# Tile 0 in written order on ScalarE, VectorE and POOL, with five weight-conversion steps per slot

## The chip, the cores and the metric

The kernel runs on one core of a Trainium2 chip. The core has five engines with a queue of instructions each: TensorE (PE; its weight loads are listed as PEld), VectorE (DVE), ScalarE (ACT), GpSimd (POOL) and SyncE (SP), which issues the DMAs. Each queue is fixed when the kernel is compiled and is worked off in its order. An instruction that waits for another engine holds what is queued behind it. The metric is the device time of one execution in microseconds.

## The reference

Three layers follow each other on 4352 tokens of width 128, all in float32.

```
phi(x)  = outer product of x@S1.T and x@S2.T            (8 x 8 = 64 features)
attn    = (phi(q) @ (phi(k).T @ v)) / (phi(q) @ sum(phi(k)) + 1e-6)   per batch and head
x       = attn / sqrt(mean(attn^2) + 1e-6) * rms_g
y       = (silu(x @ w_gate) * (x @ w_val)) @ w_out       d_ff = 1536
out     = soft mixture of 8 experts x 4 slots over all 4352 rows of y
```

Some inputs (S1, S2, w_gate, w_val and w_out) come as 64-bit floats and are handed to the kernel as pairs of 32-bit words, so that the kernel converts them to float32 on the chip.

## The kernel before

**Tiles and slots.** The rows are cut into nine tiles, eight of 512 rows and one of 256. The feed-forward layer of a tile runs over `NF = 12` slices of d_ff of 128 columns; one slice of one tile is a slot (`for i in range(n_slots + LAG)`, L947). In a slot `ff_in` (L637) makes the gate product g and the value product v on TensorE, three matmuls of 512 columns each: the high part of the weight (L621), its low part (L622), and the low part of x (L623). `ff_gate` (L647) does the silu on ScalarE and the product with v on VectorE. `ff_out` (L668), two slots later (`LAG`), multiplies with w_out into the tile's sum o. In tile 0 `ff_out` is one float32 matmul from unsplit weights, recorded as two pieces of L676; from tile 1 on it is three matmuls from split weights (L621 to L623 again), with the split of the gated value in `ff_high` and `ff_low`. The PSUM tiles of g and of v have two buffers each, so slot i+2 writes g only when the silu of slot i has read it, and v only when the gate product of slot i has.

**Weight conversion.** The weights come in nine groups in the order gv0, o0, gv1, gv2, o1, gv3, gv4, o2, gv5; a gv group serves two slots, an o group four. Converting a group takes six steps (`f64_words`, L184): ScalarE takes the absolute value of the high word (L189) and scales the low word (L192); VectorE does max, shift and or (L194, L196, L198); POOL adds the two (L202, in two pieces of 256 columns). A gv group has two more steps (`split_w`, L230): ScalarE rounds the high part (L238) and POOL subtracts it, which gives the low part wgl (L244, two pieces). The o groups get these two steps later, in `split_o`, which is appended in slot 9.

**The front.** Before the first slot `front` (L847) issues the steps of the string `FRONT` (attention for batch 0, tile 0's x, and the first 22 conversion steps) in that order on all four engines. 44 conversion steps are left for the slots: two of gv1, six of gv2, six of o1, eight of gv3, eight of gv4, six of o2 and eight of gv5. Each slot issues up to `CONV` of them.

**Order.** `in_order` (L836) runs a step, puts each of its instructions behind the latest recorded instruction of its own engine, and then records the step's last instruction of each engine in `ordered`. The edge is one of queue order and not a wait. With `ordered` and `latest` empty it does nothing, and the order on each engine is chosen by a planner, which places what its own model of the costs holds to be ready. Before, both are cleared in slot 0, so that the planner orders the slots; only conversion and chain steps of the first `LOCK = 3` slots are put behind the front (`after_front`, L892).

**Chains.** Beside the slots run generators that advance a step at a time, at two places of a slot (POST, after the gate, and PE, after `ff_out`). `q_chain(1)` makes tile 1's x: transpose L492 in slot 0, the outer products L282 and the transpose L508 in slot 1, the divides in slots 3 and 4, four squares on ScalarE and the root on POOL (L566, L567) in slot 5, the scaling L571 in slot 6, `parts` (L581, L582) in slot 8. `k_chain(1)` starts in slot 8 with POOL work (memset L324, copies L347), then transposes, projections (L354) and outer products for the keys of batch 1. `make_own` (L791 on) is POOL work that is written in tile 2.

Of the kernel before, what the change touches and what calls it, by code (L numbers as in the profile page):

```python
# [21 lines left out]
NF = DFF // P  # L22
# [12 lines left out]
qt n:4 c:1 c:1 c:1 qx kr c:2 c:2 c:2 c:2 c:2 c:2 c:3 c:3  # L35
"""

CONV = 8
LOCK = 3

WHOLE = NF
# [7 lines left out]
def body(ctx, tc, q, k, v, s1, s2, wg, wv, wo, rg, phi, w1, w2, out):  # L49
# [199 lines left out]
    def split_o():  # L249

        for i, w in enumerate(wo32):
            yield from split_w(("o", i), w, pool)
# [384 lines left out]
    def ff_in(T, f):  # L637
        w = 512 if T < 8 else 256
        for store, tag in ((gps, "g"), (vps, "v")):
            store[T, f] = [ps.tile([P, 512], F32, tag=tag, name=tag, bufs=2) for _ in pieces(T, f)]  # L640
        for e, (c, cs) in enumerate(chunks(T, f)):
            for m, store in enumerate((gps, vps)):
                o = store[T, f][e % len(store[T, f])]
                sl = slice(P * c, P * c + P)
                gate[0] = mm3(o[:, cs], wgh[:, m, sl], wgl[:, m, sl], xh[T][:, 0:w], xl[T][:, 0:w], True, True)
# [41 lines left out]
    def r_chain(T):  # L687
        x2 = row("x2")
        act.copy(x2, ops.pop(T))
        yield PE, 0  # L690
        a = aux()
        for t in range(4):
            pe.matmul(a[32 * t : 32 * t + 32, 0:P], phi_sb, x2[:, P * t : P * t + P], start=True, stop=True)
        b = aux()
        for t in range(4):
            pe.transpose(b[:, P * t : P * t + P], x2[:, P * t : P * t + P], ident)
        yield POST, 1
        lT = sb.tile([P, P], F32, tag="lT", name="lT")
        act.copy(lT, a[:, 0:P])
        act.copy(x2n[:, 4 * T : 4 * T + 4, 0:DM], b.rearrange("p (t d) -> p t d", d=DM))  # L700
        yield PE, 0
        a = aux()
        pe.transpose(a[:, 0:P], lT, ident)
        yield POST, 1
        dve.tensor_reduce(out=mcol[:, T : T + 1], in_=lT, op=ALU.max, axis=AX.X)
        dve.tensor_copy(lg[:, 4 * T : 4 * T + 4, :], a[:, 0:P].rearrange("p (t s) -> p t s", s=NS))
        if T >= 6:
            for i in range(3 if T == 6 else 1):
                yield POST, 1
                less_max(slice(8 * i, 8 * i + 8) if i < 3 and T == 6 else slice(4 * T, 4 * T + 4))  # L710
            if T == 6:
                yield POST, 1
                less_max(slice(24, 28))
# [40 lines left out]
    def a_max():  # L754

        m1 = sb.tile([P, 1], F32, tag="m1", name="m1")
        dve.tensor_reduce(out=m1, in_=mcol, op=ALU.max, axis=AX.X)
        a = aux()
        pe.transpose(a[0:1, 0:P], m1, ident)
        mr = sb.tile([P, P], F32, tag="asb", name="mr", bufs=3)[0:1].rearrange("p (t s) -> p t s", s=NS)  # L760
        m0 = a[0:1, 0:P].rearrange("p (t s) -> p s t", s=NS)
        dve.tensor_reduce(out=mr[:, 0], in_=m0, op=ALU.max, axis=AX.X)
        dve.tensor_copy(mr[:, 1:4], mr[:, 0:1].to_broadcast([1, 3, NS]))
        a = aux()
        pe.matmul(a[:, 0:NS], ones, mr[:, 0], start=True, stop=True)
        pe.matmul(a[:, NS : NS + 1], mr.rearrange("p t s -> p (t s)"), ones[:, 0:1], start=True, stop=True)
        A["m"] = sb.tile([P, 1], F32, tag="am", name="am")
        dve.tensor_copy(A["m"], a[:, NS : NS + 1])
        A["b"] = sb.tile([P, NS], F32, tag="siT", name="amb")
        dve.tensor_copy(A["b"], a[:, 0:NS])  # L770
# [43 lines left out]
    def spawn(c, phase, at=0):  # L814
        chains.append([c, phase, now + at])
# [18 lines left out]
    latest, ordered = {}, list(ENGINES)  # L834

    def in_order(step, *args):  # L836
        traced = nc.cur_bb.bb.instructions
        start = len(traced)
        with ExitStack() as s:
            for i in latest.values():  # L840
                s.enter_context(tc.issue_after(i))
            step(*args)
        for i in traced[start:]:
            if i.engine in ordered:
                latest[i.engine] = i
# [46 lines left out]
    def after_front():  # L892
        s = ExitStack()
        if now < base + LOCK:
            for i in front_end.values():
                s.enter_context(tc.issue_after(i))
        return s
# [49 lines left out]
    for i in range(n_slots + LAG):  # L947
        now = base + i
        if i < n_slots:
            T, f = slots[i]  # L950
            ff_in(T, f)
            if f == 0:
                start_tile(T)
        if i == NF - 3:
            conv.append(split_o())
        if i == 0:
            ordered.clear()
            latest.clear()
        if 1 <= i <= n_slots:
            in_order(ff_low, *slots[i - 1])  # L960
        if i < n_slots:
            in_order(ff_gate, T, f)
        for c in list(chains):
            with after_front():
                in_order(advance, POST, c)
        for _ in range(CONV):
            with after_front():
                in_order(conv_step, 1)
        if i < n_slots:
            in_order(ff_high, T, f)  # L970
        if i >= LAG:
            To, fo = slots[i - LAG]
            in_order(ff_out, To, fo)
            if fo == NF - 1 and To < 8:
                if To < 7:
                    spawn(r_chain(To), POST, 1)
                else:
                    with tc.high_priority():
                        for _ in r_chain(To):
                            pass  # L980
                        a_max()
        for c in list(chains):
            with after_front():
                in_order(advance, PE, c)
# [223 lines left out]
```

## Time and profile before

| | |
|---|---|
| median of three runs | 327.0 us (326.41 to 327.06) |
| profiled execution, its own time | 326.61 us |
| span of the profiled execution | 324.8 us |
| TensorE busy | 312.0 us, 96% |
| VectorE busy | 237.5 us, 73% |
| ScalarE busy | 185.4 us, 57% |
| POOL busy | 61.2 us, 19% |

The span is the time from the first to the last instruction; the profiled execution's own time has 1.8 us around it. Busy shares are means over the whole span and hide the stage that is changed: slot 0 begins at 23.35 us, and the last `ff_out` of tile 0 ends at 67.84 us. TensorE's durations are modelled at their ends; a 512-column matmul shows 0.39 us as a row, while the next one starts 0.23 us later.

### The profile page before, as it was taken

How to read it: one execution, taken by the hardware profiler on the slowest of the kernel's cores; microseconds unless marked ns; L12 is line 12 of the kernel's file. 1: busy time of each engine (PE TensorE's matmuls, PEld its weight loads, DVE VectorE, ACT ScalarE, POOL GpSimd, SP SyncE). 2: the span in 40 equal slices, each digit the busy share in tenths (PEclk: the TensorE clock that was granted, in tenths of full speed). 3: DMA queues.
4: the chain of work that ended last, by engine and by line, in shares of the span. 5: the costliest groups of instructions: out<-in, count | busy, mean ns of one | idle time of the engine just before them, and what ended most of it. 6: DMA issues, size and time to landing. Idle time of an engine off the chain costs nothing.

```text
span 324.8 us, 5533 instructions
## 1 busy us (share of the span) xinstructions
PE 312.0 (96%) x2028; PEld 248.1 (76%) x2028; DVE 237.5 (73%) x458; ACT 185.4 (57%) x412; POOL 61.2 (19%) x104
## 2 busy tenths in 40 slices
PE   8987989999998999999999999999999999999994
PEld 6774655778886878888888778888888878897574
DVE  4779976775878785777887868678778666664663
ACT  3757464456565455665564657565656666556553
POOL 3356699700010210001001000010020100003030
PEclk9997899999999999999999999999999999999998
DMA  8988000000007000000070000000890394000007
GB/s 201 297 289 206 0 0 1 2 0 2 0 0 199 7 2 0 2 0 0 2 198 5 3 0 2 0 0 6 279 251 3 78 339 103 0 2 0 2 3 274
DMA packets 31131, 22.40 MB, mean 69 GB/s; under 512 B 13056, under 2 KB 27136, under 8 KB 31104
## 3 DMA queue, kind: packets, MB, share of 16 engines
q1 hardware_dynamic: 31072, 22.04, 23.6%
q8 instruction: 16, 0.26, 0.3%
q14 instruction: 11, 0.09, 0.1%
q10 hardware_dynamic: 32, 0.00, 0.0%
HBM read 19.81 MB, written 2.23 MB: 68 GB/s over the span
## 4 chain that ended last, share of the span: by engine, by line
PE 75%; issue 6%; DVE 5%; DMA 1%; POOL 1%; ACT 1%; DVEq 0%; SPq 0%; POOLq 0%
PE v L621 6%; PE g L621 6%; PE v L622 6%; PE g L622 6%; PE v L623 6%; PE g L623 6%; PE o L621 6%; PE o L622 6%; PE o L623 6%; PE aux L520 3%; PE aux L384 2%; PE aux L354 2%; PE aux L497 2%; PE o L676 2%; PE fo L1159 1%
## 5 line engine op out<-in xcount | busy, mean ns | idle before, releaser
L651 ACT ACTIVATE silu<-g 128x512 f32<-128x512 f32 (+1 forms) x103 | 60.5, 592 | 41.1 <-PE g L623 38.6
L661 ACT CAST hh<-hf 128x512 fp32r<-128x512 f32 x89 | 55.0, 617 | 42.3 <-DVE hf L652 38.8
L666 DVE TENSOR_TENSOR hl<-hf,hh 128x512 fp32r<-128x512 f32 x89 | 60.9, 685 | 22.4 <-ACT hh L661 21.0
L652 DVE TENSOR_TENSOR hf<-v,silu 128x512 f32<-128x512 f32 (+1 forms) x91 | 61.8, 680 | 19.7 <-PE v L623 9.5
L621 PE MATMUL v<-xh,wgh 128*128 128x512 f32 (+1 forms) x108 | 44.0, 408 | 2.1 <-DVE hh L652 1.6
L621 PE MATMUL g<-xh,wgh 128*128 128x512 f32 (+1 forms) x108 | 42.8, 402 | 1.0 <-ACT wgh L238 1.0
L622 PE MATMUL g<-xh,wgl 128*128 128x512 f32 (+1 forms) x108 | 42.7, 395 | 0.0
L622 PE MATMUL v<-xh,wgl 128*128 128x512 f32 (+1 forms) x108 | 42.1, 390 | 0.0
L623 PE MATMUL g<-xl,wgh 128*128 128x512 f32 (+1 forms) x108 | 41.4, 384 | 0.0
L623 PE MATMUL v<-xl,wgh 128*128 128x512 f32 (+1 forms) x108 | 41.0, 381 | 0.0
L621 PE MATMUL o<-hh,woh 128*128 128x512 f32 (+1 forms) x94 | 36.8, 392 | 0.0
L623 PE MATMUL o<-hl,woh 128*128 128x512 f32 (+1 forms) x94 | 36.6, 389 | 0.0
L622 PE MATMUL o<-hh,wol 128*128 128x512 f32 (+1 forms) x94 | 35.7, 380 | 0.0
L566 POOL TENSOR_SCALAR rs<-ss 128x4 f32<-128x4 f32 (+1 forms) x9 | 2.6, 290 | 138.8 <-ACT sq L561 137.2
L621 PEld LDWEIGHTS v<-xh,wgh 128*128 128x128 f32 x108 | 20.6, 190 | 8.7 <-DVE hh L652 3.8
L621 PEld LDWEIGHTS g<-xh,wgh 128*128 128x128 f32 x108 | 20.3, 191 | 5.8 <-ACT wgh L238 1.9
L622 PEld LDWEIGHTS g<-xh,wgl 128*128 128x128 f32 x108 | 20.6, 191 | 4.7 <-issue 0.8
L622 PEld LDWEIGHTS v<-xh,wgl 128*128 128x128 f32 x108 | 20.3, 188 | 4.7 <-issue 1.3
L623 PEld LDWEIGHTS g<-xl,wgh 128*128 128x128 f32 x108 | 20.6, 191 | 4.3 <-issue 0.5
L623 PEld LDWEIGHTS v<-xl,wgh 128*128 128x128 f32 x108 | 20.3, 188 | 4.6 <-issue 0.7
L621 PEld LDWEIGHTS o<-hh,woh 128*128 128x128 f32 x94 | 17.7, 188 | 3.0
L623 PEld LDWEIGHTS o<-hl,woh 128*128 128x128 f32 x94 | 17.7, 188 | 3.0
(254 smaller groups left out, 522.2 us busy)
## 6 DMA issues: line engine op xcount, KB each, us to landing
ring<-in_moe_w_dram SPq DMA_DIRECT2D x12, 256.0 KB, 6.5
ring<-in_moe_w_dram SPq DMA_DIRECT2D x5, 512.0 KB, 5.4
ring<-in_k_dram SPq DMA_DIRECT2D x8, 256.0 KB, 3.0
qt<-in_q_dram SPq DMA_DIRECT2D x4, 512.0 KB, 5.3
ring<-in_v_dram SPq DMA_DIRECT2D x16, 128.0 KB, 4.7
ring<-in_moe_w_gate_dram SPq DMA_DIRECT2D x6, 256.0 KB, 6.3
ring<-in_moe_w_val_dram SPq DMA_DIRECT2D x6, 256.0 KB, 6.5
ring<-in_moe_w_out_dram SPq DMA_DIRECT2D x3, 512.0 KB, 6.2
```

What stands on the lines that cost most here:

```text
L354: pe.matmul(o, self.kT[g][:, P * t : P * t + pp], bdf, start=True, stop=True)
L384: pe.matmul(self.a["kv", hp][64 * h2 : 64 * h2 + D1, 64 * hp : 64 * hp + 64], va[:, h, 2 * i + g, :] if t < 8 else vr[:, h, :], self.pk[hp ...
L497: pe.matmul(self.a["q"][:, 64 * h : 64 * h + 64], self.qD[:, P * h : P * h + P], bdf, start=True, stop=True)
L520: pe.matmul(o, pD[:, f, h, :], rhs, start=(f == 0), stop=(f == 1))
L621: first = pe.matmul(o, ah, bh, start=start, stop=False)
L622: pe.matmul(o, al, bh, start=False, stop=False)
L623: last = pe.matmul(o, ah, bl, start=False, stop=stop)
L651: mark["silu"] = act.activation(s[:, cs], g[:, cs], AF.Silu).ins
L652: mark["gate", T, f] = dve.tensor_tensor(out=hf32[T, f][:, cs], in0=v[:, cs], in1=s[:, cs], op=ALU.mult).ins
L661: act.copy(hh[T, f], hf32[T, f])
L666: dve.tensor_tensor(out=hl[T, f], in0=hf32.pop((T, f)), in1=hh[T, f].bitcast(F32), op=ALU.subtract)
L676: last = pe.matmul(ops[T][:, 0:w], w_c, h[:, cs], start=(c == 0), stop=(c == NF - 1))
```

## The change

In slot 0 only TensorE is taken out of the recorded order. ScalarE, VectorE and POOL go on in written order until slot 12, the first of tile 1, where both tables are cleared. So in slots 0 to 11 each of these three queues holds, slot by slot: the silu or gate product, then what the chains issue at POST, then the conversion steps, then what the chains issue at PE. `CONV` falls from 8 to 5, so the 44 steps end in slot 8 in place of slot 5. No instruction is added or removed.

```diff
-CONV = 8
+CONV = 5
 LOCK = 3
...
         if i == NF - 3:
             conv.append(split_o())
         if i == 0:
+            ordered.remove(mybir.EngineType.PE)
+            latest.pop(mybir.EngineType.PE)
+        if i == NF:
             ordered.clear()
             latest.clear()
         if 1 <= i <= n_slots:
             in_order(ff_low, *slots[i - 1])
         if i < n_slots:
             in_order(ff_gate, T, f)
         for c in list(chains):
             with after_front():
                 in_order(advance, POST, c)
         for _ in range(CONV):
             with after_front():
                 in_order(conv_step, 1)
```

## Rows read from the trace of the kernel before

**Rows 1.** The page's 40 slices: TensorE's busy tenths and its granted clock.

```profile
PE   8987989999998999999999999999999999999994
PEclk9997899999999999999999999999999999999998
```

**Rows 2.** Busy time of each engine in four stretches of tile 0.

```profile
core 0: us, PE busy (x) PEld busy (x) DVE busy (x) ACT busy (x) POOL busy (x), PEclk, DMA share, GB/s
28.90:35.70 6.80, 6.17 (x11) 3.69 (x12) 6.77 (x13) 2.65 (x6) 3.06 (x6) 0.50 0.41 83
35.70:44.30 8.60, 8.50 (x38) 5.33 (x36) 8.50 (x15) 4.48 (x8) 7.55 (x10) 1.00 0.00 0
44.30:61.20 16.90, 15.13 (x63) 9.99 (x63) 10.88 (x16) 8.52 (x23) 16.02 (x23) 1.00 0.00 0
61.20:67.80 6.60, 6.60 (x27) 4.76 (x27) 5.30 (x10) 3.27 (x7) 1.85 (x10) 1.00 0.01 2
```

**Rows 3.** POOL's timeline (start, us, work), from gv5's add on.

```profile
52.05 1.42 POOL L202 TENSOR_TENSOR cvt<-cvs,cvc 128x256 uint32<-128x256 uint32 x2 [0.46 <-POOL rs L566]
53.41 0.98 POOL L324 MEMSET kvz<- 128x1056 f32 x1
...
55.46 1.02 POOL L567 TENSOR_TENSOR rs<-rs,mhalf 128x4 f32<-128x4 f32 x1
56.44 1.86 POOL L244 TENSOR_TENSOR wol<-ring,woh 128x256 fp32r<-128x256 f32 x2
...
59.65 1.43 POOL L244 TENSOR_TENSOR wgl<-cvt,wgh 128x256 fp32r<-128x256 f32 x2
```

**Rows 4.** TensorE's timeline at the stalls (in brackets the idle time before).

```profile
27.23 1.10 PE L497 MATMUL aux<-bd,T 128*128 128x64 f32 x8 [0.86 <-DVE T L492]
29.00 1.22 PE L621 MATMUL g<-xh,wgh 128*128 128x512 f32 x2 [0.67 <-ACT wgh L238]
...
55.00 1.03 PE L621 MATMUL g<-xh,wgh 128*128 128x512 f32 x2
...
58.48 1.00 PE L354 MATMUL aux<-bd,T 128*128 128x64 f32 x8
...
59.99 1.36 PE L354 MATMUL aux<-bd,T 128*128 128x64 f32 x10 [0.30 <-ACT T L342]
61.28 0.50 PE L622 MATMUL g<-xh,wgl 128*128 128x512 f32 x1
...
66.82 1.02 PE L676 MATMUL o<-hh,ring 128*128 128x512 f32 x2
```

**Rows 5.** The chain that ended last, two pieces: start, us, what.

```profile
54.24 0.23 PE v L622
...
54.70 0.86 PE o L676 x2
```

**Rows 6.** VectorE's timeline: conversion steps without and with POOL at work.

```profile
25.86 0.69 DVE L198 SCALAR_TENSOR_TENSOR cvs<-ring,cvt 128x512 uint32<-128x512 uint32 x1
...
31.47 0.41 DVE L194 TENSOR_SCALAR ring<-ring 128x512 f32<-128x512 f32 x1
...
48.57 0.93 DVE L194 TENSOR_SCALAR cvt<-cvt 128x512 f32<-128x512 f32 x1 [1.88 <-ACT cvt L189]
...
50.42 1.11 DVE L198 SCALAR_TENSOR_TENSOR cvs<-ring,cvt 128x512 uint32<-128x512 uint32 x1
```

**Rows 7.** Groups by shape, 23.3 to 67.8 us: busy us, mean ns, idle before.

```profile
L202 POOL TENSOR_TENSOR cvt<-cvs,cvc 128x256 uint32<-128x256 uint32 x10 | 8.2, 841 | 6.9 <-DVE cvs L198 3.7 <-ACT woh L238 2.0 <-DVE rd L536 0.7
L651 ACT ACTIVATE silu<-g 128x512 f32<-128x512 f32 x14 | 8.0, 595 | 6.8 <-PE g L623 4.8 <-DVE hh L652 1.9
L652 DVE TENSOR_TENSOR hh<-v,silu 128x512 f32<-128x512 f32 x12 | 7.9, 679 | 1.5 <-PE v L623 1.4
...
L244 POOL TENSOR_TENSOR wgl<-cvt,wgh 128x256 fp32r<-128x256 f32 x10 | 7.7, 791 | 0.0
...
L189 ACT ACTIVATE cvt<-ring 128x512 f32<-128x512 f32 x5 | 3.3, 669 | 1.8 <-POOL wgl L244 1.8
```

## The prediction, made before the changed kernel ran

> **What bounds the kernel now.** I read the page's slices first [rows 1]: TensorE is busy nearly throughout, and its granted clock dips only in the fourth and fifth slice and at the end. From tile 1 on TensorE sets the pace, so a change confined to tile 0 is worth what it makes TensorE lose there. Next the windows [rows 2]. From 28.9 to 35.7 us the granted clock is 0.50, the 1.2 GHz level, ahead of which TensorE had idled 0.86 and 0.67 us with only small matmuls between [rows 4]. VectorE is full to 44.3, then POOL, 16.0 of 16.9 us. From 61.2 TensorE is full at 2.4 GHz. So tile 0 is held by the conversion, on VectorE and then POOL, and the hand-over to the TensorE-bound part is at 61.2.
>
> POOL's timeline says why there [rows 3]. gv5's add ends at 53.5 and its high part is ready by 55.0, when the matmuls with it start [rows 4], but its subtraction runs at 59.65, behind a memset, copies, the root, another group's subtraction and more. The first matmul that wants that low part, L622 of slot 10, follows at 61.28 [rows 4]. Between 55.0 and 61.3 TensorE fills in with `ff_out` of earlier slots, tile 1's transposes and 18 key projections, 2.2 us [rows 4].
>
> **What the change moves.** It adds and removes no instruction, and it moves no DMA: the loads of batch 1 stay behind matmuls of slot 0. TensorE's order stays the planner's, but what it can do follows the other three queues. In these every instruction now holds all that is written behind it. The work that jumped ahead of gv5's subtraction (batch 1's memset and copies, the o groups' subtractions) comes behind it, which by itself gives back up to 59.65 - 53.5 = 6 us on POOL. Against that stands a new wait in each group: the cast on ScalarE waits for POOL's add, and the silus behind it on ScalarE wait too, and with them the gate products and the conversion steps behind these on VectorE. Five steps in place of eight spread the 44 steps over nine slots in place of six; by itself it puts more gates between the steps, and each silu behind fewer of them.
>
> Prices: 0.6 us for a ScalarE step (silu 0.595, L189 0.669, the next starting some 0.1 earlier), 0.68 for a gate product and the same for each other 512-column VectorE operation of the chain, twice that for the 1024-column transpose [rows 7]. An add or a subtraction is 1.42 to 1.86 for two pieces [rows 3]; I take 1.5. Max, shift and or take 0.4, 0.4 and 0.7 with POOL quiet, 0.9, 0.9 and 1.1 beside it [rows 6]: 1.5 or 2.9 us a group. The root is 1.02 plus its first half, 1.4 (estimate). The squares have no row here; four silus, 2.4 us, bound them above and nothing below, and since they are a quarter as wide I take 1.7.
>
> Worked through in queue order, with 0.1 us at each hand-over. gv1's or ends at 26.55 [rows 6]; then VectorE does gate 0, tile 1's transpose and gv2's three steps, to 29.5. POOL: gv1's add to 28.2, and behind the cast the subtraction to 30.5, then gv2's add to 32.0. ScalarE's cast of gv2 waits for that, o1's two steps follow, so the silu of slot 2 starts only at 33.75. Gate 2 ends at 35.1, o1's or at 36.4, its add at 38.0; gate 3, a divide and gv3's steps reach 39.3, gv3's add 40.9. ScalarE then does gv3's cast, gv4's two steps and silu 5, to 43.2; gate 5 to 43.9, gv4's or to 44.95. The squares end at 44.85, and since the root stands ahead of gv4's add in POOL's queue, the add ends at 47.85. The cast holds silu 6 to 49.05; gate 6, the scaling and o2's steps end at 51.75, o2's add at 53.35. Beside it VectorE does gate 7, gv5's max and shift, gate 8, tile 1's x and gv5's or, to 55.55. gv5's add ends at 57.15, its cast at 57.8, its subtraction at **59.4**, against 61.1 before (59.65 + 1.43). So the conversion comes 1.7 us earlier, and not 6: the waits in the queues cost most of what the queue-jumpers did.
>
> TensorE's side. Before, from 61.28 to the end of the last `ff_out` of tile 0 at 67.84 (66.82 + 1.02) it does 20 matmuls at 0.23 and two of 0.86 [rows 4, 5]: 8 left of slots 10 and 11, 12 of tile 1's first two slots, and two `ff_out`. After, at 59.4 the same 6.3 us are left, and besides the key projections, 2.2, which stand behind slot 9's transposes at about 59, and most of slot 9's `ff_out`, 0.6: together 9.1, so 68.5. That is **+0.7** at the full clock. The gate of slot 10 and the outer products of batch 1 on VectorE (60.7 to 63.2) run beside these matmuls.
>
> Then the clock. In this working TensorE has nothing to do from 46.4 to 48.6 (slot 8 needs gv4's cast) and from 55.1 to 57.9 (slot 10 needs gv5's), 2.2 and 2.8 us, each longer than the 0.86 and 0.67 that stood ahead of the one fall [rows 4]. That fall held 6.8 us at half clock [rows 2]. If one comes with the second gap, between 0 and 6.8 us of it lie behind 59.4, where each costs half of itself: 0 to 3.4 us. I take the middle, **+1.7**. Sum: +0.7 + 1.7 = **+2.4 us**, 326.6 + 2.4 = 329.0 against the profiled execution. The median of the runs is 0.4 above that execution, so I forecast 327.0 + 2.4 = **329.4 us**; this case's own range is 327.7 to 331.1 (+0.7 to +4.1).
>
> One price above deserves a second look: a VectorE conversion step beside POOL is up to 0.5 us dearer than alone, and the gate product is 0.68 in the mean of a stretch where POOL is mostly busy [rows 6, 7]. The Trainium skill, GPSIMD Engine Reference, section Specifications, says why it may differ: POOL shares its SBUF interfaces with VectorE, and contends with instructions in a two-port mode or with two SBUF inputs; a gate product, which reads one input from PSUM, would be spared. This trace agrees, at 0.41 against 0.93 us. By that rule every step that falls beside POOL pays, and written order would set the next group's steps beside the last one's add or subtraction; the fourth case below prices that from the rows.
>
> **The rivals.** (a) The clock stays at 2.4 GHz through the hand-over: 327.0 + 0.7 = 327.7, and with an error of 1 us either way 326.7 to 328.7. For it: between 44.3 and 61.2 TensorE idles 1.8 us in sum and keeps 1.00 [rows 2]. Against it: the gaps I expect are each longer than that whole sum.
>
> (b) Faster. The queue-jumpers were the cost, and my chain is too long. Its place is gv5's subtraction: each microsecond that it ends ahead of 59.4 is one gained, and from 58.7 on (0.7 earlier), with the clock up, the kernel is faster than before. The chain has 33 us of steps from 26.5; were each 10% shorter, the subtraction would end at 56.1, the idle stretch ahead of it would shrink, and the time is 327.0 + 0.7 - 3.3 = 324.4. For it: the root, the squares and the divides are estimates, and VectorE sits idle for some 8 us of the chain. Against it: the chain is one of waits, and hand-overs tend to add.
>
> (c) Slower yet. The steps contend with POOL throughout. I counted gv3's, gv4's and gv5's max as beside POOL and the rest mostly alone; with all of 18 steps beside it the chain grows by up to 6 groups x 1.4 us = 8 us, less the 2 counted. Half of that, 3 us, with the clock's 2.4 gives 327.0 + 0.7 + 3 + 2.4 = 333.1. For it: POOL was busy 16 of 16.9 us [rows 2]. Against it: written order leaves POOL idle while it waits for the or.
>
> That the change does nothing at all is ruled out: the planner's order before differs visibly from the written one [rows 3].
>
> **How the numbers follow.** 0.2%, or 0.65 us, is about what a measurement of this kernel can tell from no change. Chances: the forecast 0.47, (a) 0.20, (b) 0.24, (c) 0.09. The forecast and (c) are slower, 0.56; (a) splits into same 0.13, slower 0.06 and faster 0.01. So faster 0.25, same 0.13, slower 0.62. The range takes (b) at its 324.4 and (c) nearly to its 333.1, leaving about one in ten outside at each end: **324.3 to 332.8**.
>
> **What would show it.** In the trace after, gv5's subtraction should end near 59.4, with nothing of batch 1 between its add and itself; the o groups' subtractions behind it; the silu of slot 2 near 34 and of slot 6 near 49, each right behind a cast that waited for POOL; two TensorE gaps of over 2 us in the windows of 46 to 49 and 55 to 58; a second stretch at 0.50 around 55 to 65; the last `ff_out` of tile 0 at 68 to 72. From there on the traces should run in parallel to the end. The prediction is wrong if the subtraction ends ahead of 58, if the clock does not fall a second time, or if tile 1 and later change their pace.

## The result, and the profile after

The changed kernel takes 329.44 us (median of five runs, 329.32 to 331.07) against 327.0 us; the ratio is 1.0088, with a 95% interval of 1.0062 to 1.0114. It is slower by 2.4 us, which is the figure of the forecast; how much of that agreement is earned stands further down. The profiled execution is the one at 331.07: it shows a stretch at half clock at 106 to 109 us that its mean granted clock of 0.987, against 0.993 to 0.994 in the other four, sets apart, and which costs it 1.7 us (its span is 329.3 us, theirs 327.5 to 327.7). So stages up to 100 us are read from its profile, and the sum from the median.

The page's clock line, and the windows that answer to [rows 2]:

```profile
PEclk9999997999999899999999999999999999999998
```

```profile
core 0: us, PE busy (x) PEld busy (x) DVE busy (x) ACT busy (x) POOL busy (x), PEclk, DMA share, GB/s
28.90:35.70 6.80, 6.61 (x40) 5.17 (x39) 5.42 (x8) 4.18 (x9) 4.70 (x6) 1.00 0.53 111
35.70:44.30 8.60, 7.23 (x25) 3.73 (x23) 6.18 (x16) 3.84 (x9) 4.45 (x6) 1.00 0.00 0
44.30:61.20 16.90, 13.07 (x41) 8.21 (x42) 10.09 (x17) 9.37 (x22) 10.06 (x17) 0.90 0.00 0
61.20:67.80 6.60, 6.60 (x31) 4.90 (x30) 4.03 (x6) 2.23 (x7) 6.56 (x13) 1.00 0.01 2
```

Read them against [rows 2]. The early fall of the clock is gone, and 40 matmuls are recorded there in place of 11. Then it loses what it was ahead: from 44.3 to 61.2 TensorE is busy 13.07 us in place of 15.13, and no engine is full any more. POOL falls from 16.02 to 10.06, VectorE from 10.88 to 10.09. Where no engine is full and the time is longer, the time lies in waits between them. The view of who waited for whom, 28 to 62 us (total, times, longest), names them:

```profile
ACT wgh L238 <- POOL cvt L202: 15.5, 5, 4.7
DVE hh L652 <- ACT silu L651: 6.4, 2, 3.7
POOL cvt L202 <- DVE cvs L198: 4.0, 2, 2.3
```

ScalarE stands 15.5 us in front of a cast, waiting for POOL's add. One turn, in ScalarE's timeline of the changed kernel, with VectorE's gate product of slot 6 beside it:

```profile
48.50 0.62 ACT L238 CAST wgh<-cvt 128x512 fp32r<-128x512 f32 x1 [2.81 <-POOL cvt L202]
49.02 0.59 ACT L651 ACTIVATE silu<-g 128x512 f32<-128x512 f32 x1
```

```profile
45.24 0.69 DVE L198 SCALAR_TENSOR_TENSOR cvs<-ring,cvt 128x512 uint32<-128x512 uint32 x1
49.65 0.69 DVE L652 TENSOR_TENSOR hh<-v,silu 128x512 f32<-128x512 f32 x1 [3.71 <-ACT silu L651]
```

VectorE's or of gv4 ends at 45.93; POOL adds, behind the root; ScalarE casts at 48.50, then does the silu; VectorE had nothing but the gate product at the head of its queue, and idles 3.71 us. POOL's timeline, answering to [rows 3]:

```profile
56.72 1.40 POOL L202 TENSOR_TENSOR cvt<-cvs,cvc 128x256 uint32<-128x256 uint32 x2 [2.29 <-DVE cvs L198]
...
58.85 1.44 POOL L244 TENSOR_TENSOR wgl<-cvt,wgh 128x256 fp32r<-128x256 f32 x2
60.24 0.98 POOL L324 MEMSET kvz<- 128x1056 f32 x1
61.16 1.16 POOL L347 COPY va<-ring 128x512 f32<-128x512 f32 x2
...
63.42 4.19 POOL L244 TENSOR_TENSOR wol<-ring,woh 128x256 fp32r<-128x256 f32 x6
```

The queue-jumpers are gone: memset, copies and the o groups' subtractions stand behind gv5's subtraction, which ends at 60.29 (before 61.08). Of the 6 us that lay between add and subtraction in [rows 3], 0.8 came back. TensorE's timeline, answering to [rows 4]:

```profile
49.67 0.50 PE L621 MATMUL g<-xh,wgh 128*128 128x512 f32 x1 [2.44 <-ACT silu L651]
...
58.82 0.50 PE L621 MATMUL g<-xh,wgh 128*128 128x512 f32 x1 [1.39 <-ACT wgh L238]
...
68.22 1.02 PE L676 MATMUL o<-hh,ring 128*128 128x512 f32 x2
69.08 1.40 PE L354 MATMUL aux<-bd,T 128*128 128x64 f32 x10
```

TensorE is full from 58.82 on. It does the last output matmul of tile 0 at 69.24 and the last key projection by 70.3, where its next matmul starts; in the kernel before both, and nearly the same slots of tile 1, were done by 67.8 [rows 4]. A mark far behind all of this is tile 1's transposes for the router (L696), one row of TensorE's timeline in the kernel before and one after:

```profile
109.45 0.66 PE L696 MATMUL aux<-ident,x 128*128 128x128 f32 x4
```

```profile
113.47 0.66 PE L696 MATMUL aux<-ident,x 128*128 128x128 f32 x4
```

The mark is 4.0 us later, of which 1.7 is the stretch at 106; the 2.3 left is close to the 2.4 of the medians. From the mark to the end both kernels take about as long (215.4 and 215.8 us). So this row stands for the time of a kernel here to about half a microsecond, and I read it in each experiment.

### The profile page after: what moved, and what is told of

The parts are those of the page before. It is cut to its first block, busy times and chain, and to the rows that moved or that the text cites. A ratio compares the mean times of both kernels' runs of the same rounds, so it can differ in the third digit from the quotient of the medians.

```text
span 329.3 us, 5537 instructions
## 1 busy us (share of the span) xinstructions
PE 313.0 (95%) x2028; PEld 248.5 (75%) x2028; DVE 234.4 (71%) x458; ACT 184.2 (56%) x412; POOL 59.7 (18%) x104
## 4 chain that ended last, share of the span: by engine, by line
PE 78%; DVE 7%; issue 7%; ACT 3%; POOL 2%; DMA 1%; DVEq 0%; POOLq 0%; ACTq 0%; SPq 0%
PE v L621 6%; PE g L621 6%; PE g L622 6%; PE g L623 6%; PE v L622 6%; PE v L623 6%; PE o L621 6%; PE o L622 6%; PE o L623 6%; PE aux L520 4%; PE aux L384 3%; PE aux L354 2%; PE idle L296 2%; PE aux L497 2%; PE fo L1162 1%
## 5 line engine op out<-in xcount | busy, mean ns | idle before, releaser
L621 PE MATMUL g<-xh,wgh 128*128 128x512 f32 (+1 forms) x108 | 43.7, 405 | 4.2 <-ACT silu L651 2.4
L622 PE MATMUL v<-xh,wgl 128*128 128x512 f32 (+1 forms) x108 | 43.1, 399 | 0.1
L621 PE MATMUL v<-xh,wgh 128*128 128x512 f32 (+1 forms) x108 | 42.3, 392 | 0.3 <-ACT xh L581 0.3
L622 PE MATMUL g<-xh,wgl 128*128 128x512 f32 (+1 forms) x108 | 41.7, 386 | 0.1
L622 PEld LDWEIGHTS o<-hh,wol 128*128 128x128 f32 x94 | 17.9, 190 | 3.0
```

The lines of the kernel that those rows point to most:

```text
L621: first = pe.matmul(o, ah, bh, start=start, stop=False)
L622: pe.matmul(o, al, bh, start=False, stop=False)
```

## The experiments

Times are medians of the kernel named, beside runs of the kernel before on the same chip; those medians are 326.59 to 326.84 us.

**Order and step count apart.** `written8` is the written order with `CONV = 8`; `planner5` the planner's order with `CONV = 5`.

```diff
-CONV = 5
+CONV = 8
```

> The written order of the changed kernel with eight steps per slot. Theory (the chain of waits: POOL's add, the cast on ScalarE, the silu queued behind the cast, the gate product): eight steps put a whole group between two silus, so early slots take 6 us each and TensorE finds the work of slots 6 to 11 still undone when the conversion ends: 331 to 335 us. Rival (the five steps are the loss, as they spread the conversion over nine slots in place of six): 327.5 us or less.

> The kernel before with five steps per slot; the planner orders the slots. Theory: the planner places steps by readiness, so their slot matters little: 326 to 328 us. Rival (five steps are the loss): 329 us or more.

`written8`: 336.87 us, ratio 1.032 (1.0301 to 1.0339), beyond the 335 that I gave it. `planner5`: 326.69, ratio 1.0000 (0.9991 to 1.0008). So under the planner the step count is worth nothing, and the loss belongs to the written order; eight steps in written order cost four times as much as five (10.3 against 2.4 us). TensorE's stalls in `written8`:

```profile
45.02 0.79 PE L621 MATMUL g<-xh,wgh 128*128 128x512 f32 x1 [4.15 <-ACT silu L651]
...
51.88 0.50 PE L621 MATMUL g<-xh,wgh 128*128 128x512 f32 x1 [2.23 <-ACT silu L651]
...
61.03 0.50 PE L621 MATMUL g<-xh,wgh 128*128 128x512 f32 x1 [2.45 <-ACT silu L651]
```

Each waits for a silu that frees its PSUM buffer, and the silu stands behind a slot's conversion.

**One engine's order at a time.** Each of these takes further engines out of the written order in slot 0. `actfree5` is the first of them, here against the changed kernel:

```diff
-            ordered.remove(mybir.EngineType.PE)
-            latest.pop(mybir.EngineType.PE)
+            for e in (mybir.EngineType.PE, mybir.EngineType.Activation,):
+                ordered.remove(e)
+                latest.pop(e, None)
```

> The changed kernel with ScalarE's order left to the planner too; VectorE and POOL keep the written order. Theory: the silus need not queue behind a cast that waits for POOL; gv5's subtraction ends some 2 us earlier than 60.3 and the time is 326 to 328 us. Rival (the chain holds on VectorE and POOL whatever ScalarE does): 329 to 330 us.

> Only POOL keeps the written order through tile 0, with eight steps per slot. Theory: nothing of batch 1 and no subtraction of an o group stands ahead of gv5's subtraction, which ran 5.5 us after its cast in the kernel before; it ends near 56 in place of 61.1, and the time is 324.5 to 326.3 us. Rival (TensorE had other work in that stretch, so POOL's order is worth nothing): 326.4 to 327.6 us.

> Only ScalarE keeps the written order through tile 0, five steps per slot; VectorE and POOL go back to the planner. Theory (silus queued behind casts that wait for POOL): ScalarE's order alone takes the loss, 328.5 us or more. Rival (it takes the three orders together): 326 to 327.5 us.

> Only POOL keeps the written order, five steps per slot. Theory: as with eight steps, since readiness and not the slot places the steps: 324 to 325 us. Rival (the slot of a step matters for POOL's order, as the root then stands ahead of gv4's add in place of gv5's): 325.5 us or more.

> ScalarE and VectorE keep the written order, POOL goes back to the planner, five steps per slot. Theory (a loop that closes over ScalarE and VectorE: a silu stands behind the last cast, the gate product waits for the silu, the next or stands behind the gate product, the next add and cast wait for the or): the loop is still closed, 329 us or more. Rival (it takes POOL's order too): 326 to 327.5 us.

> ScalarE and POOL keep the written order, VectorE goes back to the planner, five steps per slot. Theory: the loop is open at VectorE, which can do the next group's steps ahead of a gate product that waits, and POOL has no queue-jumpers: 324.5 to 327 us. Rival (a silu behind a cast is dear whatever VectorE does): 328.5 us or more.

| written order kept by | run | us | ratio to before (95%) | L696 mark, us |
|---|---|---|---|---|
| none | planner5 | 326.69 | 1.0000 (0.9991 to 1.0008) | 109.17 |
| ScalarE | act5 | 326.96 | 1.0005 (0.9992 to 1.0019) | 109.90 |
| POOL | pool5 | 324.96 | 0.9952 (0.9940 to 0.9964) | 107.98 |
| POOL, 8 steps | pool8 | 324.36 | 0.9928 (0.9916 to 0.9941) | 107.86 |
| VectorE, POOL | actfree5 | 324.29 | 0.9924 (0.9911 to 0.9938) | 107.26 |
| ScalarE, POOL | actpool5 | 327.85 | 1.0022 (1.0006 to 1.0038) | 110.88 |
| ScalarE, VectorE | actdve5 | 330.82 | 1.0124 (1.0091 to 1.0156) | 112.26 |
| all three | the change | 329.44 | 1.0088 (1.0062 to 1.0114) | 113.47 |

Read the table by pairs. ScalarE's order added to VectorE's and POOL's costs 5.1 us (324.29 to 329.44), added to POOL's 2.9 (324.96 to 327.85), and alone nothing (`act5`, where I expected the whole loss: that form of the theory falls). POOL's order gains 1.7 us alone. Added to ScalarE's and VectorE's its medians differ by 1.4 us with overlapping intervals, and added to ScalarE's it loses 0.9, so it does not gain everywhere. VectorE's order alone was not run; added to POOL's it costs nothing (324.96 to 324.29, 1.7 us under the range that I gave `actfree5`). So at five steps the whole loss comes where ScalarE's order meets VectorE's. `actdve5` shows it without POOL's: gv5's subtraction ends only at 62.97, and TensorE idles as long as in the changed kernel, for the same releasers. Its two stalls:

```profile
49.73 0.50 PE L621 MATMUL g<-xh,wgh 128*128 128x512 f32 x1 [2.44 <-ACT silu L651]
...
58.88 0.50 PE L621 MATMUL g<-xh,wgh 128*128 128x512 f32 x1 [1.39 <-ACT wgh L238]
```

These waits fit a loop through the two queues: the silu behind the cast, the gate product behind the silu, the next or behind the gate product, the next add and cast behind the or. It is not the only path. On ScalarE the next group's first steps stand behind the cast too. In `actpool5`, where VectorE may do the next group's steps ahead of a gate product that waits, VectorE still idles 2.2 us for such a step of ScalarE, gv5's add ends at 59.70, later than the 58.12 of the changed kernel, and the time is 1 us over what I expected. How the loss divides between the two paths is not shown. Nor is ScalarE's wait by itself the loss: in `act5` the casts wait 15.0 us for POOL, nearly the 15.5 of the changed kernel, at the time of the kernel before. There TensorE did sixteen of the eighteen key projections ahead of 57.3 us; in the changed kernel all of them come after the hand-over.

With ScalarE free the waits in front of the casts shrink from 15.5 to 4.2 us, and the gate product waits for TensorE in place of the silu (`actfree5`, who waited for whom, 28 to 62 us):

```profile
DVE hh L652 <- PE v L623: 5.9, 2, 3.8
ACT wgh L238 <- POOL cvt L202: 4.2, 2, 3.1
```

The planner lets silus pass there: two run together ahead of gv4's cast, which waits for the same add of POOL as in the changed kernel. ScalarE's timeline of `actfree5`:

```profile
44.86 1.07 ACT L651 ACTIVATE silu<-g 128x512 f32<-128x512 f32 x2
47.05 0.62 ACT L238 CAST wgh<-cvt 128x512 fp32r<-128x512 f32 x1 [1.12 <-POOL cvt L202]
```

And POOL in `pool8`, where gv5's subtraction ends at 57.02, 4.1 us ahead of the kernel before, with three short pieces of `make_own` between:

```profile
52.98 1.88 POOL L202 TENSOR_TENSOR cvt<-cvs,cvc 128x256 uint32<-128x256 uint32 x2
...
55.59 1.43 POOL L244 TENSOR_TENSOR wgl<-cvt,wgh 128x256 fp32r<-128x256 f32 x2
56.95 0.98 POOL L324 MEMSET kvz<- 128x1056 f32 x1
```

Both beat the two kernels of this case, at 324.3 and 324.4 us.

**How far five steps are a choice.** `actfree8` and `actfree6` are `actfree5` with eight and six steps.

> VectorE and POOL in written order, ScalarE free, eight steps per slot. Theory (with ScalarE free, VectorE still holds each gate product behind the steps of the slot before, and eight steps hold more): slower than five steps, 325.5 to 329 us. Rival (only ScalarE's order made the step count matter): 324 to 325 us.

> VectorE and POOL in written order, ScalarE free, six steps per slot, between the runs with five (324.3) and eight (326.7). Theory (VectorE holds each gate product behind the steps of the slot before): 324.3 to 325.5 us. Rival (five is a lucky count): 326 us or more.

Eight: 326.71 us, ratio 0.9995 (0.9984 to 1.0005). Six: 329.22, ratio 1.0061 (1.0046 to 1.0075), slower than either neighbour; the rival holds. In `actfree6` TensorE stalls on a gate product late in tile 0, and the clock falls right behind, where TensorE has work. The stall, and the window of the fall:

```profile
54.33 0.50 PE L621 MATMUL v<-xh,wgh 128*128 128x512 f32 x1 [1.94 <-DVE hh L652]
```

```profile
54.90:58.30 3.40, 3.40 (x7) 1.67 (x5) 2.32 (x4) 0.62 (x2) 3.35 (x8) 0.50 0.01 2
```

`actfree5` has no such stall (its longest there is 0.67) and no fall. The traces show why six is worse, though no run tests it. The root for tile 1's x is written in slot 5. Six steps a slot finish gv4 in slot 4, so in POOL's written order the root stands behind gv4's subtraction; with five it stands ahead of gv4's add. VectorE, in written order too, holds the scaling of x (L571), and behind it gate products and gv5's steps, until the root is there. The root of `actfree5`, then the root and the scaling of `actfree6`:

```profile
44.61 1.02 POOL L567 TENSOR_TENSOR rs<-rs,mhalf 128x4 f32<-128x4 f32 x1
```

```profile
49.34 1.02 POOL L567 TENSOR_TENSOR rs<-rs,mhalf 128x4 f32<-128x4 f32 x1
```

```profile
50.40 1.21 DVE L571 TENSOR_TENSOR x<-x,rs 128x512 f32<-128x512 f32 x1 [2.95 <-POOL rs L567]
```

With eight steps the root is late as well (49.86), but VectorE had done gv5's or by 48.90 and idles 1.41 us. So the 4.9 us between five and six steps, with ScalarE free in both, are as much as any pair of the table shows. The pairs hold at five steps; what supports the reading is that the waits change with them, and differences of 1 us and less should not be read singly. TensorE's order is the planner's in all of these, and it changes with every edit.

**The clock.** `warm5` and `warm5b` are the changed kernel with spare matmuls on TensorE, whose result is not used. `warm5b`, which also puts slot 10's matmuls behind the second lot:

```diff
-            ff_in(T, f)
+            with tc.issue_after(fill[0]) if i == NF - 2 else nullcontext():
+                ff_in(T, f)
...
             in_order(ff_out, To, fo)
+            if To == 0 and fo in (5, 7):
+                warm_ps = aux()
+                with tc.issue_after(mark["mm3"]):
+                    for _ in range(18 if fo == 5 else 14):
+                        fill[0] = pe.matmul(warm_ps[:, 0:256], hot[:, 0:P], hot, start=True, stop=True).ins
```

> The changed kernel with 18 and 12 spare matmuls of 256 columns in TensorE's queue behind the output matmuls of slots 5 and 8, where it idled 2.44 and 1.39 us; their result is not used. They should hold the granted clock at 1.00 through 51.1 to 54.5 us, where the changed kernel shows 0.50. Theory (that stretch ends ahead of an idle 1.39 us that TensorE spends waiting for gv5's cast, so it costs nothing): 329 to 330 us as before the edit. Rival (the clock term of the prediction, half of the stretch): 327.5 to 328 us.

> The changed kernel with 18 and 14 spare matmuls of 256 columns in TensorE's queue behind the output matmuls of slots 5 and 7, slot 10's matmuls put behind the second lot, so that none comes after the hand-over; their result is not used. They should hold the granted clock at 1.00 from 45 us through the hand-over at 60. Theory (the changed kernel's own stretch at 0.50 costs nothing, as TensorE waits for gv5's cast behind it): 329 to 330 us. Rival (the clock term of the prediction): 327.5 to 328.3 us.

`warm5`: 331.89 us, ratio 1.0162 (1.0137 to 1.0186); neither theory. The second lot ran only behind the hand-over, at 64.3 and 65.3 us, where it took 1.3 us of a full TensorE. At the hand-over TensorE had idled 2.26 us, and from 59.7 to 63.1 the clock was at half. `warm5b`, with both lots in the gaps, holds the clock; its row and that of the changed kernel for the same 3.4 us:

```profile
51.10:54.50 3.40, 3.40 (x15) 2.20 (x14) 3.30 (x7) 2.27 (x5) 1.62 (x2) 1.00 0.00 0
```

```profile
51.10:54.50 3.40, 3.40 (x10) 2.32 (x9) 3.30 (x7) 2.17 (x5) 1.60 (x2) 0.50 0.00 0
```

Its time is 328.92 us, ratio 1.0059 (1.0047 to 1.0071), 0.5 us under the changed kernel, just below the range of the theory and above that of the rival. The 0.5 is not the fall: counted from the start of slot 0 (23.85 us in the changed kernel, 23.80 here) slot 10 starts at the same time in both, and so does the last output matmul of tile 0 (68.22 and 68.19). The start of slot 10 in `warm5b`, against 58.82:

```profile
58.77 0.50 PE L621 MATMUL g<-xh,wgh 128*128 128x512 f32 x1 [1.27 <-ACT wgh L238]
```

So in tile 0 the fall costs nothing that the traces show. About 0.4 us of the difference lies behind the row of L696 (215.8 against 215.4 us from there to the end), and its cause stays open. The other 2.1 us of the loss are there with the clock at 2.4 GHz throughout. The two runs together show what decides. The half clock at 51 to 54.5, ahead of 1.39 us that TensorE idles, moves nothing. `warm5` is 3.0 us slower than `warm5b`: 1.3 for the late matmuls, and the 1.7 left is half of the 3.4 us at half clock behind the hand-over (an estimate from these numbers).

## Why the prediction was right, and where it was not

**The chain** held. gv5's subtraction was due at 59.4 and ended at 60.29; of the 0.9, 0.5 stood already in the front (tile 0's x came at 23.11 in place of 22.61). The silu of slot 2 was due near 34 and started at 34.31, that of slot 6 near 49 and started at 49.02, each behind a cast; the o groups' subtractions came behind. One thing stood between gv5's add and subtraction after all, `make_own`'s small pieces, 0.8 us in the time of the cast. The experiments name what I had called the new wait: at five steps the whole loss needs ScalarE's and VectorE's order together, and `actpool5`, without VectorE's, keeps 1.1 us of it.

**The term of +0.7** was too small. With the clock held (`warm5b`) the loss is 2.1 us (328.92 against 326.78). In tile 0 the set of matmuls that I counted to 68.5 ends at some 69.6 (70.29, less three matmuls of a later slot), 2.0 us behind the 67.6 of before: 0.9 from the later subtraction, 0.2 from 9.3 us of work in place of 9.1, and 0.2 from one matmul that the kernel before had done beyond the set, on top of the 0.7. The front's 0.5 in it belongs to that execution; without it tile 0 ends 1.5 us later, still twice the term.

**The term of +1.7** is the step that failed. I put a fall of the clock at the second gap, with half of it behind the hand-over, because that gap would be longer than the 0.86 and 0.67 us ahead of the one fall before. The gaps came where I put them (2.44 us ahead of 49.67, 1.39 in place of 2.8 ahead of 58.82), but the clock fell after the first alone, at 51.1 to 54.5, for 3.4 us in place of 6.8, and ran at 1.00 at the hand-over: 1.39 us is longer than 0.86, and no fall followed it. The term measures nothing in tile 0, 0.5 us at the most by the medians. The early fall of the kernel before was gone, so the clock fell once in tile 0 and not a second time, which the prediction had named as a sign of being wrong; its two gaps of over 2 us were one. The two misses nearly cancel (+1.4 on the first term, -1.2 to -1.7 on this one), and so the time comes out at 329.4. That closeness is luck. The sign is earned, by the chain and the work left behind it.

**The rivals.** (a), the clock up through the hand-over, is what happened to the clock, though its 327.7 is 1.2 under the 328.92 of `warm5b`. (b), that the queue-jumpers were the cost, is right in kind for POOL alone (`pool8` gains 2.2 us; that its 324.36 meets the 324.4 is chance), and wrong for the change, which orders ScalarE too. (c) did not come: in the changed kernel most shifts and ors ran at 0.43 and 0.69, with POOL idle. Its sum was also off: it took 2.4 for the clock, the whole forecast with the 0.7 already in it, where the working gives 1.7, so by its own terms it comes to 332.4 and not 333.1.

**The two parts.** I had said that five steps put more gates between the steps and each silu behind fewer of them. In written order the step from eight to five is worth 7.4 us; under the planner it is worth nothing. What I did not separate is which queue holds the loss.

## What to carry to other kernels

A written order is a promise per queue, and it costs where a queue holds a late consumer ahead of work that is ready: ask for each engine whether an instruction that waits for another engine stands ahead of one that feeds it, and whether these waits close a loop. Fix the order of the engine whose queue is jumped, and leave free the one whose instructions wait; here POOL's order alone gained at both step counts (324.96 and 324.36 us), while with VectorE's kept too the time ran from 324.3 to 329.2 us with the count. Price a stretch at half clock by what stands behind it: here one of 3.4 us ahead of idle time moved nothing, and one where TensorE was full cost about half its length.

## What the runs showed of the hardware

The clock's stretches differ between executions of one program, and the time need not follow: two runs of the kernel before, at 326.57 and 326.53 us, had mean granted clocks of 0.986 and 0.995. Where TensorE is full the time does follow: the changed kernel's profiled execution had a stretch of 3.4 us at half clock from 105.8 us, which the mean clocks of the other four leave no room for, and was 1.6 us slower than their median. It came 1.8 us after an idle 1.38 us of TensorE (ahead of 103.96); the 1.39 us ahead of 58.82 in the same execution were followed by none. So the length of a gap did not tell whether a fall came.

The first rise of the clock also varies, from 4.1 us (`planner5`) to 7.2 us (`actfree5`) after the first instruction, and the first 21 matmuls took 3.83 and 4.66 us. Slot 0 then started at 23.22 and 24.07 us; between the profiled executions of before and after that shift was 0.5 us.
